# Weight chunks twice as wide, one scale per pair, one bias tile fewer kept, and the first attention tiles in another order

## The chip, the cores and the metric

The kernel runs on one core of a Trainium2 chip. The metric is the device time of one execution in microseconds (us); the kernel before takes 711.8 us as the median of three runs (711.26 to 712.23). Engines are called as the profile calls them: PE multiplies matrices and PEld loads its weights, DVE is VectorE, ACT is ScalarE, POOL is GpSimd, and SP issues most of the DMAs.

## The reference, cut to what matters

Attention with a learned relative bias for 4 batches, 8 heads and 576 positions of 64 numbers, then a feed-forward network (FFN) on 2304 tokens, 512 wide inside and 2048 wide in the hidden layer.

```python
scores = scale * np.matmul(q, k.transpose(0, 1, 3, 2))
x = (psi_rel / psi_i)[..., None]
h = np.maximum(x @ w1 + b1, 0.0)
bias = h @ w2
scores = scores + bias.transpose(2, 0, 1)[None, :, :, :]
...
attn = attn / (np.sum(attn, axis=-1, keepdims=True) + 1e-09)
return np.matmul(attn, v).astype(np.float32)
...
h = x @ w_in
relu6 = np.clip(h + 3.0, 0.0, 6.0)
g = h * relu6 / 6.0
return (g @ w_out).astype(np.float32)
```

The two FFN weights arrive as 64-bit floats, read as pairs of 32-bit words.

## The kernel before, in words

**Bias.** The bias table is made in 36 groups of 16 query rows. `z_group` builds four z tiles per group (a maximum on DVE, L840, or a Relu on ACT, L844), `bias_mm` multiplies them by w2 on PE (L857), `bias_out` scales the result on ACT (L873), and a DMA stores it in DRAM. `load_bias` fetches a table of 128 query rows and two heads for a softmax. `KEEP` lists tables that stay in the core's memory for all four batches.

**Weights.** `w_in_prep` and `w_out_prep` each take a weight in 16 chunks of 128 rows by 512 columns. A chunk is loaded (L244), its magnitude taken on ACT (L256), its mantissa word cleared down to the sign on POOL (L258), and the three instructions of `f64_pack` on DVE make one 32-bit float of each pair: clip with a row maximum (L273), shift and put the sign in (L277), put the low bits in (L280). Then `split_w` writes a high half on ACT (L121) and a low half on DVE (L138), both 16 bits wide. `row_scale` (L206 to L211) finds a power of two per row: for w_out per chunk, for w_in per four chunks. While w_in is packed, the memory of w_out (`wo`) holds its 32-bit floats.

**Attention.** A tile is 128 queries of one head; there are 144, numbered n, in units of four or five per pair of heads. Its scores (L520 or L542) get the bias and a row minimum on DVE (L554, `soft_max`), the exponential on ACT (L565), and a transpose. The first units of batches 0 and 1 are direct: PE transposes them (L613), and `pv_first` multiplies by v in 32-bit floats (L655).

**FFN.** `ffn` makes 16 hidden banks h_ps (L772, 12 multiplications each), a short chain on ACT and DVE after each (L762, L755, L749, L751), and four output banks o_ps (L795). The first call starts at tile 21 and waits between its halves until w_out is ready.

**Order.** The main loop writes the work tile by tile; rates in `CFG` say how many steps of w_in (`rwi`, `rw0`, `rw1`), w_out (`ro`), bias (`rb`) and FFN (`rf`) go with a tile, and how many bias groups come first (`g0`). A scheduler then orders each engine's instructions. From tile 45 on, PE keeps the written order. Each engine runs its own list strictly in order.

Of the kernel before, what the change touches and what calls it, by code (L numbers as in the profile page):

```python
# [33 lines left out]
def attention_moe_kernel(  # L34
# [212 lines left out]
    def f64_abs(t, eng):  # L247
        tv = t.rearrange("p (c w) -> p c w", w=2)
        lo, hi = tv[:, :, 0], tv[:, :, 1].bitcast(F32)
        u = pools["e"].tile([128, S], F32, tag="cu", bufs=2, name="cu")[:, 0:512]  # L250
        if eng == "Q":
            nc.gpsimd.tensor_scalar(
                out=u, in0=hi, scalar1=F64_BIAS, scalar2=1.0, op0=ALU.mult, op1=ALU.mult
            )
        else:
            nc.scalar.activation(out=u, in_=hi, func=AF.Abs, scale=F64_BIAS)  # L256
        if eng in "PQ":
            nc.gpsimd.tensor_scalar(  # L258
                out=hi, in0=hi, scalar1=0.0, scalar2=1.0, op0=ALU.mult, op1=ALU.mult
            )  # L260
        else:
            nc.scalar.activation(out=hi, in_=hi, func=AF.Copy, scale=0.0)
        return tv, u, eng == "Q"

    def f64_pack(tv, u, signed, dst, top):
        lo, sign = tv[:, :, 0], tv[:, :, 1]
# [1 line left out]
        if signed:
            nc.vector.tensor_reduce(
                out=top, in_=u, op=ALU.max, axis=AX.X, apply_absolute_value=True  # L270
            )
        else:
            nc.vector.tensor_scalar(  # L273
                out=u, in0=u, scalar1=F64_MAX, scalar2=0.0, op0=ALU.min, op1=ALU.max,
                accum_out=top,
            )
# [16 lines left out]
    def w_in_prep():  # L293
# [42 lines left out]
    def w_out_prep():  # L336
        top = const.tile([128, KF], F32, name="w2top")
        pw = const.tile([128, KF], F32, name="w2p")
        sw = const.tile([128, KF], F32, name="w2s")
# [3 lines left out]

        def pack(k, tu):
            f64_pack(*tu, None, col(top, k))
            row_scale(col(top, k), col(pw, k), col(sw, k))
            return tu[1]

        def high(k, u):
            split_w(wo[:, 0, k, :], wo[:, 1, k, :], u, col(sw, k), 0, pick("wm2", k))  # L350
            return u

        def low(k, u):
            split_w(wo[:, 0, k, :], wo[:, 1, k, :], u, col(sw, k), 1, pick("wm2", k))

        yield from staged(KF, [
            (0, lambda k, _: f64_load(w_out[k * 128:(k + 1) * 128, :], k)),
            (2, lambda k, t: f64_abs(t, pick("sg", k))), (3, pack), (4, high), (5, low),
        ])
# [82 lines left out]
    def split_v_b(b, p, u):  # L442
# [16 lines left out]
    def load_bias(b, p, i):  # L459
        out = b_p.tile([128, 2 * S], F32, tag="bt", name="bt")  # L460
        src = [out[:, s * S:(s + 1) * S] for s in range(2)]
        if (p, i) in KEEP:
# [3 lines left out]
            if tag != "cu":  # L466
                t = (const if tag[0] == "k" else pools["e"]).tile(
                    [128, 2 * S], F32, tag=tag, bufs=2 if tag == "z" else 1, name=f"k{p}{i}"
                )
                src = [t[:, s * S:(s + 1) * S] for s in range(2)]  # L470
            else:
                src = [
                    pools["e"].tile(
                        [128, S], F32, tag=tag, bufs=2, name=f"k{p}{i}"
                    )
                    for s in range(2)
                ]
# [757 lines left out]
```

## Time and profile before

| what | value |
|---|---|
| median of three runs | 711.8 us |
| profiled execution, its own time | 715.4 us |
| its span, first to last instruction | 713.6 us |
| PE busy | 660.9 us (93%) |
| DVE busy | 499.6 us (70%) |
| ACT busy | 491.6 us (69%) |
| POOL busy | 257.8 us (36%) |

Busy time is the time in which an engine has at least one instruction running. The shares are means over a span whose stages differ; the rows further below split it. A window row gives, for a stretch of the span, each engine's busy time and number of instructions, TensorE's granted clock as a share of full speed, and what the DMA engines did.

### The profile page before, as it was taken

To read this page: it belongs to the slowest core of one execution; us is meant where nothing else is said; L and a number is where in the kernel's file an instruction comes from. 1 tells how busy PE (TensorE), PEld (TensorE's weight loads), DVE (VectorE), ACT (ScalarE), POOL (GpSimd) and SP (SyncE) were. 2 spreads that over 40 slices of the span, in tenths; PEclk is the share of its full clock that TensorE was granted. 3 is DMA by queue.
4 is the path that set the end of the run, shared out by engine and by line. 5 is a ranking of instruction groups with operands and counts; after the bars stand their busy time and mean duration, and the time that the engine had idled before them with its cause. 6 is when DMAs were issued, how large, how long until landed. Compare 5 with 4: busy or idle time off the path is not lost. (4 is left out here: it accounts for less than half of the span.)

```text
span 713.6 us, 15332 instructions
## 1 busy us (share of the span) xinstructions
PE 660.9 (93%) x5538; PEld 470.7 (66%) x5538; DVE 499.6 (70%) x1263; ACT 491.6 (69%) x994; POOL 257.8 (36%) x350
## 2 busy tenths in 40 slices
PE   6557998998889998999999899999999999999998
PEld 2113665775456676788787688767776777777775
DVE  7999997889787697758867786777777776310310
ACT  6886887789576698758867786788568854630530
POOL 3212122345122154336643463465335611430420
PEclk9897999899799999999999999999999999999999
DMA  8985996456586987999999898967896765000000
GB/s 280 323 273 179 401 304 199 163 185 142 178 220 153 231 203 189 232 225 197 277 218 266 130 221 174 216 148 184 188 192 135 175 143 111 2 10 28 1 11 28
DMA packets 177500, 127.34 MB, mean 178 GB/s; under 512 B 138000, under 2 KB 146448, under 8 KB 177424
## 3 DMA queue, kind: packets, MB, share of 16 engines
q1 hardware_dynamic: 167632, 111.02, 63.5%
q10 hardware_dynamic: 9792, 15.34, 6.8%
q8 instruction: 43, 0.70, 0.4%
q14 instruction: 33, 0.27, 0.1%
HBM read 74.43 MB, written 15.34 MB: 126 GB/s over the span
## 5 line engine op out<-in xcount | busy, mean ns | idle before, releaser
L772 PE MATMUL h_ps<-x,wi 128*128 128x256 f16 (+1 forms) x1536 | 200.4, 288 | 9.9 <-DVE t L755 5.1
L795 PE MATMUL o_ps<-g,wo 128*128 128x256 f16 (+1 forms) x1536 | 196.2, 286 | 0.9 <-ACT g L121 0.8
L772 PEld LDWEIGHTS <-wi 128*128 128x128 f16 x1536 | 147.8, 98 | 57.3 <-issue 13.2
L795 PEld LDWEIGHTS <-wo 128*128 128x128 f16 x1536 | 147.2, 98 | 46.9 <-issue 10.0
L565 ACT ACTIVATE bt<-bt,sm 128x576 f32<-128x576 f32 x144 | 110.6, 768 | 57.0 <-DVE sm L554 55.5
L751 POOL TENSOR_TENSOR g<-t,g 128x256 f16<-128x256 f32 (+1 forms) x128 | 100.8, 797 | 133.1 <-ACT g L749 132.3
L138 DVE SCALAR_TENSOR_TENSOR hl<-bt,sm,hl 128x576 f16<-128x576 f32 x112 | 99.9, 902 | 26.2 <-POOL hl L115 14.6
L755 DVE SCALAR_TENSOR_TENSOR t<-t,t,h_ps 128x320 f32<-128x320 f32 (+1 forms) x112 | 56.1, 516 | 67.2 <-ACT t L762 66.3
L857 PE MATMUL b_ps<-z,w_sb 128*32 128x288 f32 x576 | 68.8, 441 | 22.5 <-ACT z L844 19.1
L115 POOL TENSOR_SCALAR hl<-bt,sm 128x576 f16<-128x576 f32 x56 | 49.7, 888 | 104.8 <-DVE sm L577 44.0
L749 ACT ACTIVATE g<-t 128x256 f16<-128x256 f32 (+1 forms) x128 | 55.5, 440 | 38.0 <-DVE t L755 37.1
L404 POOL TENSOR_TENSOR qkl<-st,qkh 128x576 fp32r<-128x576 f32 (+2 forms) x48 | 56.9, 1206 | 43.5 <-ACT qkh L397 42.2
L762 ACT ACTIVATE t<-h_ps,t,hr 128x320 f32<-128x320 f32 (+1 forms) x112 | 64.5, 587 | 7.0 <-PE h_ps L772 6.3
L554 DVE CUSTOM_DVE_ANT_0 bt<-s_ps,bt 128x576 f32<-128x576 f32 x80 | 58.8, 750 | 7.8 <-PE s_ps L542 6.7
L857 PEld LDWEIGHTS b_ps<-z,w_sb 128*32 128x32 f32 x576 | 20.5, 113 | 58.6 <-ACT z L844 32.6
L805 ACT ACTIVATE ot<-o_ps,os 128x256 f32<-128x256 f32 (+1 forms) x32 | 15.9, 497 | 57.2 <-PE o_ps L795 54.5
L840 DVE TENSOR_SCALAR z<-T,nbp 128x576 f32<-128x576 f32 x85 | 51.0, 640 | 4.6 <-PE b_ps L857 4.5
L844 ACT ACTIVATE z<-T,bp 128x576 f32<-128x576 f32 x59 | 45.2, 769 | 12.4 <-PE b_ps L857 8.6
L554 DVE CUSTOM_DVE_ANT_0 bt<-s_ps,k 128x576 f32<-128x576 f32 x64 | 46.1, 752 | 7.2 <-PE s_ps L542 5.2
L121 ACT ACTIVATE hl<-bt,sm 128x576 f16<-128x576 f32 x56 | 43.1, 769 | 7.5 <-DVE sm L577 1.9
L520 PE MATMUL s_ps<-qk 128*128 128x288 f32 x128 | 42.0, 455 | 5.9 <-DVE xr L682 3.0
L573 DVE TENSOR_SCALAR sm<-sm 128x1 f32<-128x1 f32 x112 | 16.7, 149 | 41.9 <-ACT bt L565 41.6
(118 smaller groups left out, 879.5 us busy)
## 6 DMA issues: line engine op xcount, KB each, us to landing
bt<-bias SPq DMA_DIRECT2D x32, 576.0 KB, 5.3
bias<-bo ACTq DMA_DIRECT2D x36, 288.0 KB, 4.1
w<-in_w_in_dram SPq DMA_DIRECT2D x16, 512.0 KB, 5.7
vs<-in_vp_dram SPq DMA_DIRECT2D x24, 320.0 KB, 4.9
st<-in_qk_dram SPq DMA_DIRECT2D x16, 448.0 KB, 4.0
wo<-in_w_out_dram SPq DMA_DIRECT2D x10, 512.0 KB, 7.1
bt<-bias SPq DMA_DIRECT2D x16, 288.0 KB, 3.8
k<-bias SPq DMA_DIRECT2D x7, 576.0 KB, 5.1
```

The lines of the kernel that those rows point to most:

```text
L138: nc.vector.scalar_tensor_tensor(out=out, in0=full, scalar=scale, in1=high, op0=ALU.mult, op1=ALU.subtract)
L404: nc.gpsimd.tensor_sub(out=lo[:, c:c + w], in0=t[:, c:c + w], in1=hi[:, c:c + w].bitcast(F32))
L554: nc.vector.tensor_tensor_reduce(out=halves(bt), in0=ps, in1=halves(src), op0=ALU.add, op1=ALU.min, scale=-0.125, scalar=3.0e38, accum_out ...
L565: nc.scalar.activation(out=bt, in_=bt, func=AF.Exp, scale=-1.0, bias=sm[:, 0:1], accum_out=total)
L749: nc.scalar.activation(out=g[:, 0], in_=uu, func=AF.Copy)
L751: e.tensor_sub(out=g[:, 1], in0=uu, in1=g[:, 0])
L755: nc.vector.scalar_tensor_tensor(out=t_t[f], in0=t_t[f], scalar=cols(f)[2], in1=h_t.pop(f)[:, 0:n], op0=ALU.min, op1=ALU.mult,)
L762: nc.scalar.activation(out=t_t[f], in_=h_t[f][:, 0:n], func=AF.Relu, scale=cols(f)[0], bias=cols(f)[1],)
L772: nc.tensor.matmul(out=h_t[f][:, 0:n], lhsT=wi[:, a, c, f * 128:(f + 1) * 128], rhs=x[:, e, c], start=(k == 0), stop=(k == 3 * KC - 1),)
L795: nc.tensor.matmul(out=ops[:, 0:n], lhsT=wo[:, a, f, e * 128:(e + 1) * 128], rhs=g_t[f][:, r], start=(f == 0 and a == 0 and r == 0), stop= ...
L840: nc.vector.tensor_scalar(out=z, in0=src, scalar1=nbp[:, col], scalar2=None, op0=ALU.max)
L857: nc.tensor.matmul(out=pss[a][32 * k:32 * k + 32, 0:HALF], lhsT=w2_sb, rhs=z[:, a * HALF:(a + 1) * HALF],)
```

## The change

Both weights are taken in half as many chunks of twice the size: w_in in 8 chunks of 1024 columns, w_out in 8 pairs of 128-row chunks. Each instruction of the packing and splitting covers 1024 columns. A pair of w_out chunks shares one scale per row, so the tables that hang on it have 8 columns instead of 16. The loads of w_in go through two buffers of 2048 words in place of five of 1024. w_in is packed in place in `wo`; for w_out the working tile is `cu` or the kept-tile slot `kb1`, and its loads go to both planes of a quarter of `wo` or to `z_e`.

The z tiles of the bias are two fixed tiles, `z_e` and `z_a`, each for a whole group. Bias table (2, 1) is not kept any more; batches 1 to 3 load it again. The first eight tiles go two by two over head pairs 0 and 1. Eight bias groups come ahead of the loop in place of 16, the others two at a time inside it; w_in's and w_out's rates are lower at first. `pv_first` takes a bank of the pool that h_ps uses in place of the pool of the scores.

```diff
-CFG = {'z0': 'AD', 'gz': 12, 'z1': 'AD', 'gz2': 16, 'zeng': 'DDA', 'sg': 'P', 'wm1': 'A', 'wm2': 'A', 'hl': 'AP', 'gl': 'PP', 'vm': 'A', 'g0': 16, 'rwi': 3.0, 'rw0': 1.0, 'rw1': 1.3, 'ro': 1.3, 'rb': 1.7, 'rf0': 1.3, 'rf': 2.0, 'rf1': 1.55, 'la': 6, 'gq': 2, 'gap': 0.0, 'wu': 8, 'act': 'o', 'w64': 5, 'rfo': 2.3, 'tv': 'A', 'pw': 0, 'po': 0, 'gr': 'AD', 'wb': 3, 'fb': 2, 'spn': 45, 'sw': 45, 'bo': 16, 'rb0': 1.5}
+CFG = {'z0': 'AD', 'gz': 12, 'z1': 'AD', 'gz2': 16, 'zeng': 'DDA', 'sg': 'P', 'wm1': 'A', 'wm2': 'A', 'hl': 'AP', 'gl': 'PP', 'vm': 'A', 'g0': 8, 'rwi': 2.0, 'rw0': 0.3, 'rw1': 0.7, 'ro': 0.85, 'rb': 1.7, 'rf0': 1.3, 'rf': 2.0, 'rf1': 1.55, 'la': 6, 'gq': 2, 'gap': 0.0, 'wu': 8, 'act': 'o', 'g1': 2, 'w64': 5, 'rfo': 2.3, 'tv': 'A', 'pw': 0, 'po': 0, 'gr': 'AD', 'wb': 3, 'fb': 2, 'spn': 45, 'sw': 45, 'ws': 2, 'os': 11, 'ro2': 2.0, 'bo': 12, 'rb0': 1.5}
...
-            t = pools["w"].tile([128, 1024], U32, tag="w64", bufs=cfg["w64"], name="w64")
-        elif k < 8 or k in (10, 11):
-            a, c = k % 2, 8 + 4 * (k // 2 % 2)
-            t = wo[:, a, c:c + 4, :].rearrange("p k e -> p (k e)").bitcast(U32)
+            t = pools["w"].tile([128, 2048], U32, tag="w64", bufs=2, name="w64")
+        elif k % 3 == 2 or k == 7:
+            t = z_e.bitcast(U32)[:, :, 0:1024]
         else:
-            t = pools["e"].tile([128, 2 * S], U32, tag="z", bufs=2, name="w64")[:, 0:1024]
+            c = 8 + 4 * (k % 3 if k < 6 else 1)
+            t = wo[:, :, c:c + 4, :].rearrange("p a k e -> p a (k e)").bitcast(U32)
...
         def at(k):
-            return k // 4, slice(512 * (k % 4), 512 * (k % 4) + 512)
+            return k // 2, slice(1024 * (k % 2), 1024 * (k % 2) + 1024)
...
-        yield from staged(16, [
-            (0, load), (2, lambda k, t: f64_abs(t, pick("sg", k))), (3, pack), (7, high), (8, low),
+        yield from staged(8, [
+            (0, load), (1, sign), (2, pack),
+            (4, lambda k, _: split(k, 0)), (5, lambda k, _: split(k, 1)),
         ])
...
+        def split(k, u):
+            ks = slice(2 * k, 2 * k + 2)
+            for step in range(2):
+                split_w(wo[:, 0, ks, :], wo[:, 1, ks, :], u, col(sw, k), step, pick("wm2", k))
+
+        ws = cfg["ws"]
+        yield from staged(KF // 2, [
+            (0, load_early), (ws - 1, load_late), (ws, sign), (ws + 1, pack), (ws + 2, split),
         ])
...
-        (0, 1): "kb0", (2, 1): "kb1",
+        (0, 1): "kb0",
...
-    tiles = [(b, p, t) for b, p, u in units for t in UT[u]]
+    tiles = [(0, p, t) for ts in ((0, 1), (2, 3)) for p in range(2) for t in ts]
+    tiles += [(b, p, t) for b, p, u in units[2:] for t in UT[u]]
...
-        ps = s_bank("pv_ps")
+        ps = halves(w_bank("pv_ps"))
...
-            fs = slice(f, f + 1)
+            fs = slice(f // 2, f // 2 + 1)
...
+                z2 = (z_a if phase == 0 and g % 2 else z_e)[:, k // 2]
...
-            bias_until(256 if i < 2 else S)
+            bias_until(128 * i + 128 if i < 2 else S)
...
+        for _ in range(cfg["g1"]):
+            if emitted[0] < 16:
+                bias_next()
...
-            ao[0] += cfg["ro"]
+            ao[0] += cfg["ro"] if out_steps[0] < cfg["os"] else cfg["ro2"]
```

The start of attention, on DVE: the rows that stand around the first softmax (`bt,sm<-s_ps,bt`) of the kernel before. `w_438` to `w_494` are loaded chunks of w_in, z is the bias, `wo` is w_in's 32-bit form and `w1p`, `w1s` its scales.

```order
L277 SCALAR_TENSOR_TENSOR cu<-cu,w_466 128x512
L313 TENSOR_REDUCE w1top<-w1parts 128x1
L280 SCALAR_TENSOR_TENSOR wo<-w_466,cu 128x512
L206 TENSOR_SCALAR w1p<-w1top 128x1
L840 TENSOR_SCALAR z<-T,nbp 128x576
L273 TENSOR_SCALAR cu,w1parts<-cu 128x512
L161 TENSOR_SCALAR w1p<-w1p 128x1
L277 SCALAR_TENSOR_TENSOR cu<-cu,w_494 128x512
L211 RECIPROCAL w1s<-w1p 128x1
L273 TENSOR_SCALAR cu,w1parts<-cu 128x512
L280 SCALAR_TENSOR_TENSOR wo<-w_494,cu 128x512
L554 ISA bt,sm<-s_ps,bt 128x576
```

The same place of the changed kernel, on DVE, where `w_276` and `w_341` are the third and fourth of the eight wide chunks of w_in.

```order
L263 TENSOR_SCALAR wo,w1parts<-wo 128x1024
L266 SCALAR_TENSOR_TENSOR wo<-wo,w_276 128x1024
L139 SCALAR_TENSOR_TENSOR wi<-wo,w1s,wi 128x1024
L837 TENSOR_SCALAR z_a<-T,nbp 128x576
L269 SCALAR_TENSOR_TENSOR wo<-w_276,wo 128x1024
L139 SCALAR_TENSOR_TENSOR wi<-wo,w1s,wi 128x1024
L554 ISA bt,sm<-s_ps,bt 128x576
L554 ISA sm 128x1
L263 TENSOR_SCALAR wo,w1parts<-wo 128x1024
L178 TENSOR_REDUCE vparts<-vf 128x1
L837 TENSOR_SCALAR z_e<-T,nbp 128x576
L266 SCALAR_TENSOR_TENSOR wo<-wo,w_341 128x1024
```

The first softmax moved from behind 13 of w_in's 16 chunks to behind three of its eight; the rest of w_in now stands between the first tiles.

The end of w_in and the start of w_out, on DVE, in the kernel before: `wi` is w_in's finished halves, and the clip into `w2top` is the first of w_out.

```order
L138 SCALAR_TENSOR_TENSOR wi<-wo,w1s,wi 128x512
L554 ISA bt,sm<-s_ps,bt 128x576
L554 ISA sm 128x1
L138 SCALAR_TENSOR_TENSOR wi<-wo,w1s,wi 128x512 x2
L157 COPY p_v_773<-m_ps 128x1
L157 COPY p_w_794<-m_ps 128x1
L138 SCALAR_TENSOR_TENSOR wi<-wo,w1s,wi 128x512
L273 TENSOR_SCALAR cu,w2top<-cu 128x512
```

The same place of the changed kernel, on DVE.

```order
L139 SCALAR_TENSOR_TENSOR wi<-wo,w1s,wi 128x1024 x2
L158 COPY p_v_777<-m_ps 128x1
L162 TENSOR_SCALAR p_v_777<-p_v_777 128x1
L184 RECIPROCAL s_v_780<-p_v_777 128x1
L682 TENSOR_TENSOR xr<-pv_ps,xr 128x256
L554 ISA bt,sm<-s_ps,bt 128x576
L554 ISA sm 128x1
L682 TENSOR_TENSOR xr<-pv_ps,xr 128x256
L554 ISA bt,sm<-s_ps,bt 128x576
L554 ISA sm 128x1
L153 TENSOR_REDUCE g_w_858<-m_ps 1x1
L263 TENSOR_SCALAR cu,w2top<-cu 128x1024 x2
```

The first w_out chunk stood right behind w_in's last half. The first two wide chunks of w_out now stand ten rows behind it; their loads go to both planes of `wo`, where w_in's last two 32-bit chunks lie until that last row of `wi` has read them.

The seventh chunk of w_in, `w_572`, on DVE in the changed kernel. It is loaded into the buffer of `w_431`, the fifth; the rows begin with the instruction that reads `w_431` last.

```order
L269 SCALAR_TENSOR_TENSOR wo<-w_431,wo 128x1024
L139 SCALAR_TENSOR_TENSOR wi<-wo,w1s,wi 128x1024
L158 COPY p_v_626<-m_ps 128x1
L139 SCALAR_TENSOR_TENSOR wi<-wo,w1s,wi 128x1024
L263 TENSOR_SCALAR wo,w1parts<-wo 128x1024
L162 TENSOR_SCALAR p_v_626<-p_v_626 128x1
L266 SCALAR_TENSOR_TENSOR wo<-wo,w_485 128x1024
L305 TENSOR_REDUCE w1top<-w1parts 128x1
L184 RECIPROCAL s_v_629<-p_v_626 128x1
L269 SCALAR_TENSOR_TENSOR wo<-w_485,wo 128x1024
L207 TENSOR_SCALAR w1p<-w1top 128x1
L263 TENSOR_SCALAR wo,w1parts<-wo 128x1024
```

In the kernel before, a chunk's buffer came free four chunks ahead of its use; now it is one chunk ahead, and the last row above needs the load and its magnitude on ACT.

## Rows read from the trace of the kernel before

**Rows 1.** Windows: stretch in us, busy time (instructions), clock, DMA share, GB/s

```profile
0.00:61.00 61.00, 39.99 (x280) 12.73 (x280) 54.78 (x128) 48.50 (x72) 14.70 (x28) 0.92 0.84 281
61.00:118.00 57.00, 51.55 (x313) 35.07 (x314) 53.58 (x165) 45.19 (x93) 11.21 (x20) 0.94 0.77 271
118.00:206.00 88.00, 77.92 (x560) 53.90 (x557) 75.36 (x206) 64.84 (x130) 34.94 (x43) 0.90 0.64 191
...
240.00:604.00 364.00, 351.80 (x3294) 270.74 (x3294) 272.87 (x666) 270.20 (x583) 165.47 (x220) 1.00 0.88 193
604.00:714.00 110.00, 106.37 (x796) 76.27 (x793) 20.00 (x38) 38.95 (x78) 25.28 (x32) 0.99 0.05 16
```

**Rows 2.** Chain that ended last: start us, us, what

```profile
684.29 26.09 PE o_ps L795 x192
```

**Rows 3.** Who waited for whom, DVE, 61 to 240 us: total, times, longest

```profile
DVE vparts L177 <- DMA va<-in_vp_dram: 5.8, 3, 2.5
DVE wo L138 <- ACT wo L121: 4.3, 4, 2.0
```

**Rows 4.** Timeline of DVE, 65 to 69 us: start us, us, instruction

```profile
65.12 0.69 DVE L280 SCALAR_TENSOR_TENSOR wo<-w,cu 128x512 uint32<-128x512 uint32 x1
65.73 0.74 DVE L138 SCALAR_TENSOR_TENSOR wi<-wo,w1s,wi 128x512 f16<-128x512 f32 x1
66.39 0.68 DVE L273 TENSOR_SCALAR_CACHE_REDUCE cu<-cu 128x512 f32<-128x512 f32 x1
...
67.00 0.68 DVE L273 TENSOR_SCALAR_CACHE_REDUCE cu<-cu 128x512 f32<-128x512 f32 x1
...
67.60 1.29 DVE L277 SCALAR_TENSOR_TENSOR cu<-cu,w 128x512 uint32<-128x512 uint32 x2
```

**Rows 5.** Instructions of single lines on DVE: ns min/median/max, first and last start

```profile
L273 DVE TENSOR_SCALAR_CACHE_REDUCE cu<-cu x32: 665/674/686, 9.7 to 174.4; 128x512 f32<-128x512 f32 x32
L273 DVE DVE_READ_ACCUMULATOR cu<-cu x32: 71/81/84, 10.4 to 175.0; 128x1 f32 x32
L277 DVE SCALAR_TENSOR_TENSOR cu<-cu,w x22: 672/685/1149, 11.5 to 176.7; 128x512 uint32<-128x512 uint32 x22
L280 DVE SCALAR_TENSOR_TENSOR wo<-w,cu x16: 671/680/693, 13.6 to 72.3; 128x512 uint32<-128x512 uint32 x16
L138 DVE SCALAR_TENSOR_TENSOR vl<-vs,s_v,vh x24: 872/885/1383, 169.7 to 590.1; 128x640 f16<-128x640 f32 x24
L138 DVE SCALAR_TENSOR_TENSOR wi<-wo,w1s,wi x16: 734/744/1152, 29.1 to 79.9; 128x512 f16<-128x512 f32 x16
```

**Rows 6.** Timeline of DVE, small instructions at 182.6 us

```profile
182.62 0.16 DVE L211 RECIPROCAL w2s<-w2p 128x1 f32<-128x1 f32 x1
182.69 0.14 DVE L577 RECIPROCAL sm<-sm 128x1 f32<-128x1 f32 x1
```

**Rows 7.** Line L256 on ACT: ns min/median/max, first and last start

```profile
L256 ACT ACTIVATE cu<-w x22: 649/672/685, 9.0 to 169.3; 128x512 f32<-128x512 f32 x22
```

**Rows 8.** Line L244, loads of 512 KB: us from issue to landing

```profile
DMA to landing us min/median/max: 3.5/5.8/10.1
```

**Rows 9.** Timeline of SP and of ACT: a pair of w_out loads and their first reader

```profile
80.50 1.69 SPq L244 DMA_DIRECT2D wo<-in_w_out_dram  x2
...
87.71 1.24 ACT L256 ACTIVATE cu<-wo 128x512 f32<-128x512 f32 x2 [0.22 <-DMA wo<-in_w_out_dram]
```

**Rows 10.** FFN lines L772 (95 to 200 us) and L795: ns, first and last start

```profile
L772 PE MATMUL h_ps<-x,wi x192: 269/273/421, 99.8 to 182.8; 128*128 128x256 f16 x192
...
L795 PE MATMUL o_ps<-g,wo x1536: 269/291/310, 203.9 to 710.1; 128*128 128x256 f16 x96, 128*128 128x320 f16 x96
```

**Rows 11.** DMA issues: KB each, median us to landing

```profile
bt<-bias SPq DMA_DIRECT2D x32, 576.0 KB, 5.3
```

**Rows 12.** Who waited for whom, PE, 240 to 604 us: total, times, longest

```profile
PE s_ps L542 <- DVE sm L554: 4.9, 5, 1.6
PE h_ps L772 <- DVE x L138: 4.7, 3, 2.8
```

More of the change, by code (lines that the diff above doesn't have):

```diff
@@ L245, in f64_load, with f64_abs, f64_pack @@
         return t
[L247 to L254, printed above, removed]
-        else:
[L256 to L266, printed above, removed]
-        ub = u.bitcast(U32)
[L268 to L276, printed above, removed]
+    def f64_abs(t, u):
+        if len(t.shape) == 3:
+            tv, u = t.rearrange("p a (c w) -> p a c w", w=2), u.rearrange("p (a c) -> p a c", a=2)
+            lo, hi = tv[:, :, :, 0], tv[:, :, :, 1].bitcast(F32)
+        else:
+            tv = t.rearrange("p (c w) -> p c w", w=2)
+            lo, hi = tv[:, :, 0], tv[:, :, 1].bitcast(F32)
+        nc.scalar.activation(out=u, in_=hi, func=AF.Abs, scale=F64_BIAS)
+        nc.gpsimd.tensor_scalar(
+            out=hi, in0=hi, scalar1=0.0, scalar2=1.0, op0=ALU.mult, op1=ALU.mult
+        )
+        return lo, hi.bitcast(U32), u
+    def f64_pack(lo, sign, u, top):
+        ub = u.bitcast(U32)
+        nc.vector.tensor_scalar(
+            out=u, in0=u, scalar1=F64_MAX, scalar2=0.0, op0=ALU.min, op1=ALU.max, accum_out=top,
+        )
         nc.vector.scalar_tensor_tensor(
@@ L296, in w_in_prep @@
         )
-        parts = const.tile([128, 16], F32, name="w1parts")
+        parts = const.tile([128, 8], F32, name="w1parts")
         top = const.tile([128, KC], F32, name="w1top")
@@ L336, in w_out_prep, with load, load_early, load_late @@
     def w_out_prep():
-        top = const.tile([128, KF], F32, name="w2top")
-        pw = const.tile([128, KF], F32, name="w2p")
-        sw = const.tile([128, KF], F32, name="w2s")
+        top = const.tile([128, KF // 2], F32, name="w2top")
+        pw = const.tile([128, KF // 2], F32, name="w2p")
+        sw = const.tile([128, KF // 2], F32, name="w2s")
         def col(t, k):
             return t[:, k:k + 1]
+        def load(k):
+            src = w_out[256 * k:256 * k + 256, :].rearrange("(a p) e -> p a e", a=2)
+            return f64_load(src, k)
+        def load_early(k, _):
+            return load(k) if k < 6 else None
+        def load_late(k, t):
+            return load(k) if k >= 6 else t
+        def sign(k, t):
+            if k % 2:
+                u = const.tile([128, 2 * S], F32, tag="kb1", name="cu")
+            else:
+                u = pools["e"].tile([128, 2 * S], F32, tag="cu", name="cu")
+            u = u[:, 0:1024]
+            return (*f64_abs(t, u), u)
         def pack(k, tu):
-            f64_pack(*tu, None, col(top, k))
+            f64_pack(*tu[:3], col(top, k))
             row_scale(col(top, k), col(pw, k), col(sw, k))
[L347 to L358, printed above, removed]
+            return tu[3].rearrange("p (k e) -> p k e", k=2)
+        def split(k, u):
[5 more added lines that the diff above has]
+            (0, load_early), (ws - 1, load_late), (ws, sign), (ws + 1, pack), (ws + 2, split),
         ])
@@ L361, in w_out_prep @@
         for name, c in (("t3", 3.0 * CQ), ("t6", 6.0 * CQ)):
-            t = const.tile([128, KF], F32, name=name)
+            t = const.tile([128, KF // 2], F32, name=name)
             nc.vector.tensor_scalar(
@@ L465, in load_bias @@
             tag = KEEP[p, i]
-            if tag != "cu":
+            if tag == "z":
+                t = z_e[:, p // 2]
+            else:
                 t = (const if tag[0] == "k" else pools["e"]).tile(
-                    [128, 2 * S], F32, tag=tag, bufs=2 if tag == "z" else 1, name=f"k{p}{i}"
+                    [128, 2 * S], F32, tag=tag, name=f"k{p}{i}"
                 )
[L470 to L477, printed above, removed]
+            src = [t[:, s * S:(s + 1) * S] for s in range(2)]
             kept[p, i] = src
@@ L1031, in attention_moe_kernel @@
     if cfg["wu"]:
-        wz = pools["a"].tile([128, 2 * S], F32, tag="z", bufs=1, name="wz")[:, 0:S].bitcast(F16)
+        wz = z_a[:, 1, 0:S].bitcast(F16)
         nc.vector.memset(wz, 0.0)
```

42 lines of the change are left out of this document (19 added, 23 removed).

## The prediction

> **What bounds the kernel now.** I read the windows first, cut where the profile changes. In the last stretch PE is busy throughout, and from 240 to 604 us PE is busy 97% of the time [rows 1]. The chain of waits names the same engine: its last piece is 192 output multiplications in 26.09 us, 0.136 us each, with no gap [rows 2]. So from about 240 us on the end is set by how much PE work is left and when it is taken up. Before that it is not: in the first 118 us DVE is busy 54.78 of 61.00 and 53.58 of 57.00 us, PE 39.99 and 51.55, ACT less than DVE. From 118 to 206 us DVE (75.36 of 88.00) and PE (77.92) wait in turns [rows 1]. The granted clock there is 0.90 to 0.94 of full speed, so PE's busy time is partly spent at the lower level of 1.2 GHz, yet PE is waited for less than DVE. What the change saves on DVE before some 206 us therefore starts PE's long stretch earlier, nearly one for one up to 118 us; what it only moves between engines does not.
>
> **The wide instructions.** Packing and splitting are 32 each of L273, L277, L280 and L138 on DVE; they become 16 of twice the width. DVE's next instruction starts 0.61 us after L280, 0.66 after L138 and 0.61 after L273 with its readout, and two of L277 take 1.29, or 0.645 each [rows 4]. Together that is 2.525 us per chunk. The added 512 columns I price by the two widths of L138: 885 ns for 640 columns, 744 for 512, or 1.10 ns a column, 0.56 us per instruction [rows 5]. Widening four instructions costs 2.26, so a pair of chunks saves 0.27 us and 16 pairs 4.3. Of the scale instructions (three per w_out chunk) 24 go. Such a small one keeps the next waiting 0.07 us [rows 6], so 1.7 us. The lower end is 6.0 us. If each instruction's whole duration counted, a pair would save 0.674 + 0.081 + 0.685 + 0.680 + 0.744 less 2.26, or 0.60 us, 16 pairs 9.7 us [rows 5], and 24 small ones at 0.15 us 3.6 [rows 6]: 13.3 us. I take 8, nearer to the starts, since DVE is almost never idle where most of the packing stands; some of it stands where the next instruction does wait.
>
> The two rows of L277 show an overlap: 1.29 us for two of 0.685. The Trainium skill (VectorE: DVE Perf Modes, section "The DRAIN you can't avoid") says that the next instruction does not start until the one before has left the pipe, and that leaving out semaphores does not help. By that rule the saving would be the upper end, 13.3 us, and the sum below 12.2 us; the trace disagrees for these instructions, so the rule is only a rival.
>
> Beside this, DVE's low half waits for ACT's high half in w_out, 4.3 us in 4 waits [rows 3]. With half as many chunks I take 2.1 us off; the bounds are 0 and 4.3. ACT loses 32 fixed parts and POOL 16, but both have more idle time than DVE in these stretches [rows 1]: nothing, as DVE's own list covers it.
>
> **The wider loads.** This is what the change adds. A load of 512 KB took 3.5, 5.8 or 10.1 us (least, median, most) [rows 8]. A load of 1 MB is not in the trace. The nearest row is a pair of 512 KB loads issued at 80.50 whose reader on ACT had to wait 0.22 us for them, until 87.71: 7.2 us for 1 MB [rows 9]. From below it is 3.5 us and 1.9 more for the second half at 271 GB/s [rows 1, 8], or 5.4; from above 10.1 and 1.9, or 12.0. I take 7.2. Then ACT takes the magnitude, at most twice 0.672, or 1.3 us [rows 7]. So DVE gets a chunk 8.5 us after its buffer was free (6.7 to 13.3).
>
> With two buffers in place of five, what stands in DVE's list in between has to cover that. For the seventh chunk of w_in these are two halves at 1.22, three packing rows at 1.17, 1.21 and 1.17, and five small ones at 0.07: 6.3 us, so DVE waits 2.2. ACT's list is blocked as well: its reader stands ahead of exponentials, and PE's transposes wait for those. For the first pair of w_out, the eighth half (1.22) and ten instructions stand in between; at the stretch's mean of 53.58/165, or 0.32 us [rows 1], they cover 4.5 us, and DVE waits 4.0. The last pair of w_out goes through a buffer that came free late too; I count 2.2, as for w_in. Together 8.4 us. I take half, 4.2: DVE idles 3.4 us from 61 to 118 and 12.6 from 118 to 206 as it is [rows 1], and while it waits for a load the other engines catch up on what it would have waited for next. The bounds are 0 and, with loads of 12.0 us and nothing caught up, 7.0 + 8.8 + 7.0 = 22.8.
>
> The row for 512 KB is what this kernel's loads take beside each other. The Trainium skill (DMA: Bandwidth & Descriptors, section "Anatomy of one DMA — SWDGE (gpsimd) path") gives 2.0 us and the bytes at 436 GB/s, for another issuing path; by it I estimate 4.4 us for 1 MB, waits of 1 us after halving, and a sum 3 us lower. The trace disagrees: by the same formula 512 KB would take 3.2 us, and its median is 5.8.
>
> **What is moved.** The first softmax goes ahead of most of w_in. DVE was full either way, so the order alone gives nothing there: 0, with the packing behind it as the cover. It would count if PE or ACT were late for DVE; they have 17 and 15 us to spare in the first 118 us by their idle sum less DVE's [rows 1].
>
> After the last attention tile the changed order leaves 732 FFN multiplications in place of 780. These 48, at 0.136 us, are 6.5 us of PE work pulled forward. It pays only where PE would have waited: for scores 4.9 us, for x 4.7 between 240 and 604 us [rows 12]. PE's list is strict, so most waits stay; I take 1 us, bounds 0 and 6.5.
>
> The edits I cost at nothing: the first FFN call's 192 hidden multiplications are spread from 99.8 to 182.8 us, 5.2 us for each of 16 banks [rows 10], so `pv_first` in one of two banks does not hold them up; without that cover, four stays of some microseconds each. The table that is no longer kept comes back as three loads of 576 KB and 5.3 us [rows 11], asked for several tiles ahead; uncovered, 16 us. The fixed z tiles hold two groups where the pools held one and a half; the remaining 20 bias groups start some tiles later but end by the same tile.
>
> **The sum**, against the profiled execution's own 715.4 us (span 713.6 and 1.8 around it): -8.0 packing, -2.1 waits for ACT, +4.2 loads, -1.0 tail, or -6.9: 708.5. That execution stands 3.6 us above the median of 711.8; from the median, 704.9 us.
>
> **Rivals.** *A larger gain.* The fixed parts come off in full (-13.3), the waits for ACT go (-4.3), loads land early (+1.5) and the tail gives 2: -18.1, 693.7 us. For it: DVE is the fullest engine for 118 us. Against: the overlapping starts [rows 4].
>
> *Nothing.* The saving is that of the starts, -6.0 - 2.1, and the three waits for loads count in full, +8.4: 712.1 us. For it: nothing in DVE's list stands ready where it waits. Against: DVE's idle time before 206 us.
>
> *Slower.* One mechanism: the 1 MB loads through two buffers. It decides once a load takes over 10 us: then, even halved, 3 times 11.4 less the covers of 6.3, 4.5 and 6.3 come to 8.6, which is what packing and waits give. At 12.0 us, not halved, +22.8 - 8.1: 726 us. For it: 10.1 us for half the size did occur [rows 8]. Against: the pair in 7.2 us [rows 9], and 271 to 281 GB/s is moved in these stretches with DMA engines 77 to 84% busy [rows 1], so there is some room.
>
> **Chances.** My forecast, from 700 to 710.4 us, gets 0.50; the larger gain 0.20; nothing 0.12; slower 0.18. A measurement of this kernel can tell about 0.2%, 1.4 us, from no change. So faster 0.70, the same 0.12, slower 0.18. The extremes of all terms at once are 688 and 729; the range from 693 to 715 leaves out about 0.05 below and 0.13 above. The forecast's own range is 700 to 710.4.
>
> **What would show it.** The 1024-column packing rows would last about 1.2 to 1.3 us; with 1.1 the larger gain is on. Loads of w_in should land in about 7 us, and DVE's waits should show two or three of some microseconds ahead of a clip, with ACT's magnitude as the releaser; with none, that term falls. The 40 us after the end of w_in's packing should be shorter than before by less than the packing saves. The first output multiplication of the first FFN call, at 203.9 us before [rows 10], should come some 6 us earlier, and from there on the two traces should run in parallel. I am wrong if that point is as early as predicted and the end is not, or if DVE has idle time of 15 us more than before ahead of it.

## The result, and the profile after

The changed kernel takes 703.45 us (median of 4 runs, 701.48 to 705.12) against 711.72; the ratio is 0.988, 95% interval 0.9855 to 0.9906. Forecast were 704.9 and a range of 693 to 715. A later measurement gave 0.991 (0.9887 to 0.9933). The two profiles exaggerate: the execution of before lies 3.7 us above its median, that of after (701.48, span 699.5) 2.0 below, so they are 13.9 us apart where the medians are 8.3. Places and orders are read from them; sizes go by the medians.

The windows of the changed kernel, cut where [rows 1] are, with the same columns:

```profile
0.00:61.00 61.00, 40.85 (x318) 17.98 (x318) 52.73 (x108) 51.31 (x71) 13.13 (x22) 0.94 0.86 297
61.00:118.00 57.00, 50.86 (x301) 34.01 (x302) 47.83 (x120) 41.17 (x76) 10.61 (x15) 0.94 0.77 271
118.00:206.00 88.00, 78.96 (x617) 56.86 (x616) 78.81 (x182) 70.86 (x133) 41.31 (x39) 0.94 0.65 193
...
240.00:604.00 364.00, 352.76 (x3292) 270.81 (x3290) 270.48 (x662) 272.25 (x585) 159.15 (x224) 1.00 0.86 189
604.00:714.00 110.00, 92.07 (x691) 65.99 (x688) 14.37 (x27) 30.27 (x60) 19.75 (x25) 0.99 0.04 13
```

DVE is busy 8 us less in the first 118 us and 3.5 more from 118 to 206. From 240 to 604 us PE, DVE and ACT differ by at most 2.4 us (POOL by 6.3), so the time was won before 240 and kept. The end is the chain of [rows 2], only earlier:

```profile
669.99 26.09 PE o_ps L795 x192
```

What was won is hardly idle time of PE. The first row of each page, before and after:

```profile
PE 660.9 (93%) x5538; PEld 470.7 (66%) x5538; DVE 499.6 (70%) x1263; ACT 491.6 (69%) x994; POOL 257.8 (36%) x350
PE 647.4 (93%) x5538; PEld 469.3 (67%) x5538; DVE 487.8 (70%) x1159; ACT 488.6 (70%) x963; POOL 252.7 (36%) x334
```

PE is idle for 52 to 53 us in both (713.6 less 660.9, 699.5 less 647.4). Its busy time is 13.5 us shorter for the same 5,538 multiplications. The granted clock of the whole span is 0.973 and 0.980 in these two executions, by an estimate 5 us of it, about what they exaggerate. For the rest: a multiplication's record lasts 0.27 us (the median of L772 further down), yet in an unbroken row a new one comes every 0.136 us ([rows 2], 26.09 us for 192). So multiplications that stand closer together show as less busy time.

The packing and splitting lines on DVE, after; they answer [rows 5]:

```profile
L263 DVE TENSOR_SCALAR_CACHE_REDUCE wo<-wo x8: 1185/1206/1219, 12.7 to 72.2; 128x1024 f32<-128x1024 f32 x8
L266 DVE SCALAR_TENSOR_TENSOR wo<-wo,w x8: 1208/1219/1226, 14.0 to 74.1; 128x1024 uint32<-128x1024 uint32 x8
L269 DVE SCALAR_TENSOR_TENSOR wo<-w,wo x8: 1203/1216/1221, 16.0 to 77.3; 128x1024 uint32<-128x1024 uint32 x8
L139 DVE SCALAR_TENSOR_TENSOR wi<-wo,w1s,wi x8: 1261/1274/1283, 30.3 to 82.8; 128x1024 f16<-128x1024 f32 x8
```

How soon the next instruction starts, in the changed kernel's timeline of DVE at 70 and at 93 to 98 us; it answers [rows 4]:

```profile
70.17 1.28 DVE L139 SCALAR_TENSOR_TENSOR wi<-wo,w1s,wi 128x1024 f16<-128x1024 f32 x1
71.37 0.16 DVE L662 TENSOR_SCALAR r_sb<-r_sb 128x4 f32<-128x4 f32 x1
...
93.55 1.22 DVE L263 TENSOR_SCALAR_CACHE_REDUCE cu<-cu 128x1024 f32<-128x1024 f32 x1
94.69 0.08 DVE L263 DVE_READ_ACCUMULATOR cu<-cu 128x1 f32 x1
...
95.37 1.23 DVE L266 SCALAR_TENSOR_TENSOR cu<-cu,wo 128x1024 uint32<-128x1024 uint32 x1
96.52 0.14 DVE L207 TENSOR_SCALAR w2p<-w2top 128x1 uint32<-128x1 uint32 x1
...
96.71 1.21 DVE L269 SCALAR_TENSOR_TENSOR cu<-wo,cu 128x1024 uint32<-128x1024 uint32 x1
97.85 0.14 DVE L162 TENSOR_SCALAR w2p<-w2p 128x1 f32<-128x1 f32 x1
```

And in the kernel before, the row behind the two of L277 at 67.60, the last of [rows 4]:

```profile
68.81 0.15 DVE L313 TENSOR_REDUCE w1top<-w1parts 128x1 f32<-128x4 f32 x1
```

In the changed kernel the next starts come 1.20, 1.14, 1.15 and 1.14 us later: 4.63 per wide chunk. The row of the kernel before corrects the prediction: two of L277 hold the next back for 1.21 us, not for 1.29, which reaches to the end of the second. That is 0.605 each, so a narrow chunk takes 2.485 and two take 4.97. Sixteen times 0.34 is 5.4 us, and with the 24 small instructions' 1.7 it is 7.1, where 8 was taken.

Loads of the weights, 1 MB each, after; 7.2 us were taken from [rows 9]:

```profile
DMA to landing us min/median/max: 4.9/6.9/9.7
```

Who made DVE wait in the changed kernel, 61 to 240 us (total, times, longest), of the rows that have to do with the weights; it answers [rows 3]:

```profile
DVE wo L139 <- DMA wo<-in_w_out_dram: 1.7, 1, 1.7
...
DVE wo L139 <- ACT wo L122: 1.5, 2, 1.1
...
DVE cu L263 <- ACT cu L255: 0.8, 1, 0.8
```

Waits for ACT's high half fell from 4.3 to 1.5 us. Two small waits have to do with loads here (1.7 for a load of w_out, 0.8 for a magnitude on ACT), and before 61 us one of 0.5.

The first FFN call, after, against [rows 10]: its hidden multiplications end five microseconds sooner, its first output multiplication starts 12.4 us sooner, and the last one of all 14.3 sooner.

```profile
L772 PE MATMUL h_ps<-x,wi x192: 269/273/421, 103.0 to 177.8; 128*128 128x256 f16 x192
...
L795 PE MATMUL o_ps<-g,wo x1536: 269/292/310, 191.5 to 695.8; 128*128 128x256 f16 x96, 128*128 128x320 f16 x96
```

### The profile page after: what moved, and what is told of

It reads as the page before. It is cut to its first block, busy times and chain, and to the rows that moved or that the text cites. A ratio compares the mean times of both kernels' runs of the same rounds, so it can differ in the third digit from the quotient of the medians.

```text
span 699.5 us, 15122 instructions
## 1 busy us (share of the span) xinstructions
PE 647.4 (93%) x5538; PEld 469.3 (67%) x5538; DVE 487.8 (70%) x1159; ACT 488.6 (70%) x963; POOL 252.7 (36%) x334
## 5 line engine op out<-in xcount | busy, mean ns | idle before, releaser
L772 PE MATMUL h_ps<-x,wi 128*128 128x256 f16 (+1 forms) x1536 | 202.6, 290 | 8.6 <-DVE t L755 3.9
L795 PE MATMUL o_ps<-g,wo 128*128 128x256 f16 (+1 forms) x1536 | 195.5, 286 | 0.8 <-DVE g L120 0.4
L772 PEld LDWEIGHTS <-wi 128*128 128x128 f16 x1536 | 149.2, 99 | 56.2 <-issue 13.9
L795 PEld LDWEIGHTS <-wo 128*128 128x128 f16 x1536 | 147.3, 98 | 46.0 <-issue 8.3
L751 POOL TENSOR_TENSOR g<-t,g 128x256 f16<-128x256 f32 (+1 forms) x128 | 102.5, 810 | 135.9 <-ACT g L749 134.9
L116 POOL TENSOR_SCALAR hl<-bt,sm 128x576 f16<-128x576 f32 x56 | 45.0, 805 | 105.6 <-DVE sm L577 59.6
L554 DVE CUSTOM_DVE_ANT_0 bt<-s_ps,bt 128x576 f32<-128x576 f32 x88 | 64.8, 749 | 10.0 <-PE s_ps L542 5.2
L854 PE MATMUL b_ps<-z_e,w_sb 128*32 128x288 f32 x448 | 44.1, 430 | 9.9 <-ACT bo L870 4.2
L520 PE MATMUL s_ps<-qk 128*128 128x288 f32 x128 | 40.2, 439 | 7.3 <-ACT atf L616 2.6
L837 DVE TENSOR_SCALAR z_e<-T,nbp 128x576 f32<-128x576 f32 x69 | 37.8, 595 | 5.4 <-PE b_ps L854 5.4
L841 ACT ACTIVATE z_e<-T,bp 128x576 f32<-128x576 f32 x43 | 32.0, 767 | 7.9 <-PE b_ps L854 4.1
L542 PE MATMUL s_ps<-qkh 64*128 64x288 f32 x192 | 30.4, 346 | 6.6 <-DVE sm L554 6.3
L870 ACT ACTIVATE bo<-b_ps,cv_sb,isc 128x576 f32<-128x576 f32 (+1 forms) x47 | 33.2, 709 | 4.2 <-DMA at<-hl 2.2
```

The lines of the kernel that those rows point to most:

```text
L116: nc.gpsimd.tensor_scalar(out=out, in0=full, scalar1=scale, scalar2=1.0, op0=ALU.mult, op1=ALU.mult)
L542: nc.tensor.matmul(out=s_t[n + j][:, a, 0:HALF], lhsT=w[q], rhs=m[rows, cs], start=(k == 0), stop=(k == 2),)
L554: nc.vector.tensor_tensor_reduce(out=halves(bt), in0=ps, in1=halves(src), op0=ALU.add, op1=ALU.min, scale=-0.125, scalar=3.0e38, accum_out ...
L751: e.tensor_sub(out=g[:, 1], in0=uu, in1=g[:, 0])
L772: nc.tensor.matmul(out=h_t[f][:, 0:n], lhsT=wi[:, a, c, f * 128:(f + 1) * 128], rhs=x[:, e, c], start=(k == 0), stop=(k == 3 * KC - 1),)
L795: nc.tensor.matmul(out=ops[:, 0:n], lhsT=wo[:, a, f, e * 128:(e + 1) * 128], rhs=g_t[f][:, r], start=(f == 0 and a == 0 and r == 0), stop= ...
```

## Experiments

All were timed beside the kernel before, on three chips: it gave 712.17 us beside runs one to four, 712.86 beside five to eight and 712.82 beside the last four. Ratios are to it, so that kernels of different chips can be compared. Where code is changed, the scheduler also places some instructions anew before tile 45, so such a run changes more than its edit says.

**The changed kernel again**, unedited.

> The changed kernel itself, as the mark for the three kernels beside it on the same chip. It gave 703.45 us, 8.3 under the kernel before; I expect 7 to 10 under it again.

Measured: 705.71 us, ratio 0.991 (0.9887 to 0.9933), 6.5 under before.

**DVE's instructions as halves.**

```diff
-            low_part(lo, t, scale, hi)
+            for a in range(2):
...
+                low_part(h[0], h[1], scale, h[2])
...
+        for a in range(2):
+            nc.vector.scalar_tensor_tensor(
+                out=half(ub, a), in0=half(ub, a), scalar=3, in1=half(sign, a),
...
+            nc.vector.scalar_tensor_tensor(
+                out=half(ub, a), in0=half(lo, a), scalar=29, in1=half(ub, a),
...
```

Here `h` holds the halves of the low half's operands, and `half(t, a)` is the a-th 512 columns of t.

> The changed kernel with three of the four wide DVE instructions of each weight chunk (both bit operations and the low half) issued as two of 512 columns; loads, ACT, POOL and buffers stay. Theory one (DVE's fixed parts before some 200 us set the end): by the starts of before (0.645, 0.61, 0.66 us) against those of after (1.14, 1.14, 1.20), 0.35 us per chunk and 5.6 for 16; with 48 instructions at DVE's fullest place I expect 3 to 5.6 us of it at the end. If the pipe's emptying were paid by every instruction: 0.50 per chunk, 8 us. Rival (the new order of the first tiles made the gain, DVE had slack left after it): under 1.5 us.

Measured: 712.32 us, ratio 1.0016 (0.9996 to 1.0035): 6.6 us slower than the first run. That is the whole gain, for 48 instructions. With L277 at 0.605 the price by starts is 4.3, not 5.6 (0.27 us per chunk); 6.6 lies between it and the price by full durations (8).

**FFN steps across the last attention tile.** In the changed kernel, and with the sign reversed in the kernel before:

```diff
+        if n == SWITCH + 1:
+            credit -= 4.0
         if queue:
```

`credit` counts the FFN steps owed to the loop.

> The changed kernel with four FFN steps (48 multiplications, 6.5 us of PE) put off from the attention part to behind its last tile, so that 780 are left there as in the kernel before. Theory one (PE is busy at both places, and work moved between them changes little): 0 to 2 us slower, 1 as predicted. Rival (the 48 multiplications pulled forward fill waits of PE): 5 to 6.5 us slower, most of the gain.

> The kernel before with four FFN steps more taken up from tile 46 on, so that 732 multiplications are left behind the last attention tile as in the changed kernel; nothing else changes. Theory one: 0 to 2 us faster than before. Rival: 5 to 6.5 us faster.

Measured: 704.71 us (0.9896, 0.986 to 0.9933), and 711.47 (0.9998, 0.9975 to 1.002). Neither differs from its partner; by the medians both are a little faster, 1.0 and 0.7 us. Work moved between two stretches in which PE is busy is worth next to nothing.

**The old start.** The tile order, how far ahead bias tables are loaded (`la`) and the bias rows wanted are put back as well.

```diff
-'g0': 8, 'rwi': 2.0, 'rw0': 0.3, 'rw1': 0.7, ... 'g1': 2
+'g0': 16, 'rwi': 3.0, 'rw0': 0.6, 'rw1': 0.7, ... 'g1': 0
-    tiles = [(0, p, t) for ts in ((0, 1), (2, 3)) for p in range(2) for t in ts]
...
+    tiles = [(b, p, t) for b, p, u in units for t in UT[u]]
```

> The changed kernel (wide chunks, pairs, two load buffers, fixed z tiles) with the start as before: 16 bias groups ahead of the loop, seven of w_in's eight chunks packed before the first softmax, the first eight tiles in the old order. Theory one (the gain is DVE's fixed parts; the order alone gives nothing, as predicted): 0 to 2 us slower than the changed kernel, 704 to 708 us. Rival (the early first softmax made the gain): 710 us or more.

Measured: 715.07 us, 1.0041 (1.0016 to 1.0065), 9.4 slower than the first run and slower than before. My theory fails: the rival holds. The start is not quite the old one: in the trace five of w_in's eight chunks, not seven, are packed ahead of the first softmax, which starts at 49.9 us (36.9 in the first run, 61.2 in the kernel before).

**ACT and POOL as halves.**

```diff
+            for a in range(2):
...
+                high_part(h[0], h[1], scale, mode)
...
+        for a in range(2):
+            nc.scalar.activation(out=half(u, a), in_=half(hi, a), func=AF.Abs, scale=F64_BIAS)
+            nc.gpsimd.tensor_scalar(
+                out=half(hi, a), in0=half(hi, a), scalar1=0.0, scalar2=1.0, op0=ALU.mult, op1=ALU.mult
+            )
```

> The changed kernel with the magnitude and high half on ACT and the sign on POOL issued as two of 512 columns each; DVE's instructions stay wide. 32 more on ACT (2 x 0.672 us against 1.15 for the magnitude, some 6 us in all), 16 more on POOL. Theory one (only DVE is waited for there): 0 to 1.5 us slower. Rival (each chunk is a chain through ACT, POOL and DVE, so any of them counts): 3 to 6 us slower.

Measured: 710.74 us, 0.9973 (0.9947 to 1.0000), 5 slower by the medians, 4.5 by the ratios. That is the rival's number, on engines costed at nothing; whether by the rival's mechanism is not shown.

**The scale of w_out sooner**, an entry of `CFG` alone.

```diff
-'ro2': 2.0
+'ro2': 4.0
```

> The changed kernel with w_out's last steps, the row scale of all of w_out among them, taken four per tile in place of two (a rate of the table alone). In the changed kernel 21 us lie between w_out's last low half and the first output multiplication, 12 of them before the transposition of the scale. Theory one (this bridge decides when PE's long stretch begins): the first output multiplication 3 to 8 us earlier and the end 1 to 4 us earlier. Rival (PE has scores and hidden multiplications enough in the bridge): within 1 us.

Measured: 715.54 us, 1.0044 (1.0018 to 1.007), 9.8 slower. Neither theory had that.

**w_out sooner.**

```diff
-'ro': 0.85
+'ro': 1.0
```

> The changed kernel with w_out's first steps at one per tile in place of 0.85, so that its packing ends some two tiles sooner and the bias groups follow sooner too. Theory one (the end hangs on when w_out is ready): 1 to 5 us faster. Rival (DVE is full there, so what is pulled ahead pushes attention back by as much): within 1.5 us.

Measured: 703.38 us, 0.9868 (0.9844 to 0.9891): 2 to 3 us faster than the first run, with intervals that still touch.

By then two entries of `CFG` had moved the end by 10 us one way and 2 the other, with the same instructions. What their traces differ in most plainly is where PE has FFN work. A row here gives the first and the last start in the stretch. The seventh run, first call's hidden half, its output half, and the second call's hidden half:

```profile
L772 PE MATMUL h_ps<-x,wi x192: 269/273/418, 103.9 to 178.6; 128*128 128x256 f16 x192
...
L795 PE MATMUL o_ps<-g,wo x192: 272/273/421, 190.1 to 219.5; 128*128 128x256 f16 x192
...
L772 PE MATMUL h_ps<-x,wi x192: 272/273/421, 244.8 to 271.8; 128*128 128x256 f16 x192
```

Two gaps, 11.5 us (178.6 to 190.1) and 25.3 (219.5 to 244.8), in which PE has only attention and bias. The same for the last version below, where they are 3.3 and 6.6:

```profile
L772 PE MATMUL h_ps<-x,wi x192: 269/273/283, 101.7 to 180.0; 128*128 128x256 f16 x192
...
L795 PE MATMUL o_ps<-g,wo x192: 269/273/284, 183.3 to 215.5; 128*128 128x256 f16 x192
...
L772 PE MATMUL h_ps<-x,wi x192: 269/273/283, 222.1 to 256.4; 128*128 128x256 f16 x192
```

The gaps of all, read from such rows, with the granted clock from 175 to 210 us in the same profiled execution (us, us, share, us):

| kernel | first gap | second gap | clock | median |
|---|---|---|---|---|
| before (profiled execution) | 21.1 | 2.3 | 0.85 | 711.7 |
| changed, first run | 13.5 | 8.2 | 0.95 | 705.7 |
| DVE halves | 24.8 | 7.7 | 0.77 | 712.3 |
| FFN steps later | 13.3 | 8.0 | 0.95 | 704.7 |
| before, FFN steps ahead | 22.2 | 2.3 | 0.95 | 711.5 |
| old start | 22.2 | 10.0 | 0.82 | 715.1 |
| ACT and POOL halves | 22.2 | 7.9 | 0.80 | 710.7 |
| scale sooner | 11.5 | 25.3 | 0.85 | 715.5 |
| w_out sooner | 3.3 | 17.8 | 1.00 | 703.4 |
| DVE halves, w_out sooner | 3.6 | 18.8 | 1.00 | 709.9 |
| old start, w_out sooner | 5.2 | 19.2 | 1.00 | 715.8 |
| both gaps closed | 3.3 | 6.6 | 1.00 | 699.4 |
| before, w_out sooner | 5.3 | 12.0 | 1.00 | 708.4 |

So a new theory: the gaps (holes, in the expectations) are the price, whatever opens them. The last four runs try it with each suspect, the first gap closed by the rate of w_out.

**DVE halves and w_out sooner**: both edits above.

> DVE's three instructions as halves (as in the second run), with w_out's first steps at one per tile. Over the runs so far the end goes with the hole between the first FFN call's last hidden and first output multiplication: 13.7 us in the changed kernel, 3.3 with w_out sooner, 22 to 25 in the three slower variants and 21 before. Theory hole: with w_out sooner the hole closes here too, and the halves cost 0 to 2.5 us against the 703.4 of w_out sooner: 703 to 706. Theory DVE (the fixed parts themselves are the gain): 5 to 7 us, 708.5 to 710.5.

Measured: 709.87 us, 0.9962 (0.9943 to 0.9982), 6.5 slower than w_out sooner. The first gap is 3.6 us, and yet the price is the same as in the second run: gaps are not the whole price, and the number is the one that the theory of DVE's fixed parts gave.

**Old start and w_out sooner**: both edits above.

> The old start (16 bias groups ahead, seven w_in chunks before the first softmax, old tile order) with w_out's first steps at one per tile. Theory hole: the old start lost 9 to 11 us because the first output multiplication fell behind three more tiles; here it does not, so 703 to 707. Rival (the early softmax itself is the gain): 710 us or more.

Measured: 715.8 us, 1.0049 (1.0028 to 1.007), 12.4 slower than w_out sooner, with a first gap of 5.2. Again not the gap.

**Both gaps closed.**

```diff
-'ro': 0.85, ... 'sw': 45
+'ro': 1.0, ... 'sw': 42
```

> The changed kernel with w_out's first steps at one per tile and the switch to four FFN banks at tile 42 in place of 45, so that the second FFN call begins three tiles sooner. With w_out sooner alone the first hole is 3.3 us but 17.8 us lie between the first call's last output and the second call's first hidden multiplication. Theory hole: that closes to under 8 us, and the end comes 3 to 6 us sooner, 697 to 701. Rival (attention and bias fill PE there as well): 702 to 705.

Measured: 699.38 us, 0.9806 (0.978 to 0.9832), faster than both kernels and 4.0 faster than w_out sooner, as the theory of gaps expected: same instructions, both gaps under 7 us.

**The kernel before, w_out sooner.**

```diff
-'ro': 1.3
+'ro': 1.5
```

> The kernel before with w_out's steps at 1.5 per tile in place of 1.3; nothing else changes. Its hole is 21 us. Theory hole: the first output multiplication follows the hidden ones within 10 us and the end comes 3 to 8 us sooner, 704 to 709, without wide chunks. Rival (in the kernel before DVE is too full to have w_out ready sooner, which is what the wide chunks changed): within 2 us of before.

Measured: 708.43 us, 0.9934 (0.9913 to 0.9955). Some 4.4 us of the 8 could be had without wide chunks, by a rate that closed the first gap of the kernel before from 21.1 to 5.3 us.

Among the four kernels with the change's own instructions and start, a line through scale sooner (36.8 us of gaps) and both gaps closed (9.9) rises 0.60 us per microsecond; it puts the first run (21.7) at 706.5 and w_out sooner (21.1) at 706.1, where 705.7 and 703.4 were measured. That is an estimate: two points fix the line, and the other two lie at almost the same place. So gaps are one price, and what the halves and the old start cost comes beside it.

## Why the prediction was right, point by point

**What bounds.** Right as to the place: the end moved by what was won before 240 us, and PE's work after that is unchanged. The signs named for it came out: the first output multiplication is 12.4 us earlier where 6 were expected (the profiles exaggerate, by 5.6 us at the end), and the last one 14.3; ahead of the first DVE idles 24.6 us in place of 22.3, far from 15 more. What the prediction did not see is the form: PE waits no less in all, its multiplications stand closer together.

**The wide instructions, -8.** The size is right, by rows 7.1. By runs, undoing three of the four cost 6.6 and 6.5 us, where their starts alone give 4.3; DVE's busy time grew by 3.6 and 4.8 us (487.5 to 491.1 and 492.2 to 497.0). The upper rival (each instruction paid in full until the pipe is empty; the Trainium skill, VectorE: DVE Perf Modes, section "The DRAIN you can't avoid") would have asked for 8; by that rule's price the runs lie in between, but the rows after show the overlap again, 1.14 us to the next start of an instruction of 1.22. So some 2 us of the price are not DVE's own time, and the new placing is in it too: the first hidden multiplication comes at 110.0 us in place of 102.9, and at 110.8 in place of 102.7. Where it is lost shows from the softmax of tile 32 to that of tile 48 (first run, second run, w_out sooner, DVE halves and w_out sooner):

```profile
143.90:249.10 105.20, 95.28 (x850) 67.47 (x850) 83.34 (x206) 76.32 (x143) 38.98 (x42) 0.95 0.77 197
143.50:258.80 115.30, 102.51 (x846) 71.77 (x846) 86.25 (x220) 79.22 (x145) 36.89 (x44) 0.88 0.69 178
144.20:253.80 109.60, 102.40 (x909) 71.44 (x912) 83.14 (x211) 81.16 (x152) 41.06 (x45) 0.96 0.71 182
144.20:259.90 115.70, 103.79 (x914) 71.81 (x916) 88.97 (x227) 84.05 (x154) 38.53 (x46) 0.97 0.69 172
```

Tile 32 comes no later with the halves. Behind it the stretch is 10.1 and 6.1 us longer, with DVE busy for 2.9 and 5.8 more. In the second run's execution the clock fell from 0.95 to 0.88 as well, in the ninth it did not, so the same price was not lost in quite the same way.

**ACT and POOL at nothing.** Unproven, and likely wrong. Halving their instructions cost 4.5 to 5 us. The trace of that run has a first gap of 22.2 us in place of 13.5, which the line above would price at about 5; whether the fixed parts opened it or the scheduler's new placing did was not separated. Late packing did not open it: w_out's last low half starts at 169.4 us there and at 171.6 in the first run. The 2.1 us for ACT's high half came as 2.8.

**The wider loads, +4.2.** The landing was right (6.9 us median for 7.2), the size too large. Three waits of 2.2, 4.0 and 2.2 us were expected, 8.4 before halving. Those that name a load or a magnitude are 0.5, 0.8 and 1.7, or 3.0 in all. DVE idles more all the same, in the windows up to the 20th and the 32nd tile's softmax, before and after:

```profile
0.00:114.00 114.00, 87.54 (x557) 45.22 (x558) 105.70 (x280) 90.50 (x157) 25.91 (x48) 0.93 0.81 278
114.00:159.00 45.00, 41.95 (x295) 31.66 (x293) 36.64 (x106) 34.03 (x71) 16.45 (x21) 0.92 0.63 210
```

```profile
0.00:106.00 106.00, 81.34 (x554) 44.94 (x555) 88.57 (x204) 83.84 (x131) 21.55 (x35) 0.94 0.82 289
106.00:144.00 38.00, 33.33 (x234) 25.12 (x231) 37.70 (x76) 32.06 (x60) 18.75 (x15) 1.00 0.73 256
```

DVE idles 17.4 us up to tile 20 in place of 8.3; from there to tile 32 it idles 0.3 in place of 8.4. The net is 1 us at tile 32. Of the 9.1 more up to tile 20 only the 3.0 stand at loads of the weights. The rest stands mainly at a bias table (2.7), at `xr`, of which the FFN's input x is made (2.8), and at scores (2.0), work of attention that the new order put there. No run tried the loads alone, so what they cost stays open.

**What is moved, 0.** This step failed: "the order alone gives nothing there". Putting the old start back costs 9.4 and 12.4 us, more than the whole change gives. The reason given was that DVE was full either way. But with the old start tile 32 comes only 1.8 us later than in the first run (145.7 and 143.9 us), and tile 48 comes 11.5 later (260.6 and 249.1). With w_out sooner they are 2.6 later (146.8 and 144.2) and 11.8 later (265.6 and 253.8). So most is lost behind tile 32, where DVE is not full. From the softmax of tile 32 to that of tile 48, old start, and old start with w_out sooner:

```profile
145.70:260.60 114.90, 103.27 (x863) 72.97 (x864) 81.81 (x202) 79.25 (x147) 38.66 (x44) 0.90 0.69 177
146.80:265.60 118.80, 107.38 (x930) 75.72 (x933) 85.10 (x207) 84.02 (x156) 40.55 (x48) 0.94 0.65 167
```

Beside the same stretch of their partners above, DVE is busy for 1.5 us less and 2.0 more, and PE for 8.0 and 5.0 more, with 13 and 21 more multiplications and a clock of 0.90 for 0.95 and 0.94 for 0.96. The first gap goes with it in the one pair (22.2 us in place of 13.5) and hardly in the other (5.2 and 3.3). What in the old start does that to those tiles stays open.

**The tail, -1.** Not told from nothing: moving the 48 multiplications across the last tile changed neither kernel beyond the noise. The rival's 5 to 6.5 us are excluded.

**The sum.** It came out through terms that cancel. DVE's halves (6.6) and the start (9.4) together exceed the 6.5 us of the first run, so the two are not independent, or the rest of the change costs some 10 us: wide chunks with the old start are slower than before. Two load buffers, the fixed z tiles, the table loaded again and the bank of `pv_first` were not tried one by one, nor the new start with narrow chunks, so which of them costs or earns what is open. A rate in `CFG` alone moved the end by 2 to 10 us, so a price of 5 us from a run that also places instructions anew is no clean price of its edit. The range and the sign were earned; the closeness of 704.9 was in part luck.

## What to carry to other kernels

Price a wide instruction by the start of the next one at both widths, read to the next row and not to the end of a merged one; here the runs cost 2 us more than that. Do not cost a new order at nothing because the fullest engine stays full: ask where the strict engine, here PE, will lack its long independent work, and read the gaps between its stages. Such a gap can be worth as much as the edit, and a rate may close it: two numbers in `CFG` gave 6 us here.

## What was not expected of the hardware

TensorE's granted clock fell inside such gaps although PE was busy for most of them. PE, from 175 to 210 us, in the second run, the seventh, and the last version (both gaps closed):

```profile
175.00:210.00 35.00, 31.40 (x212) 17.89 (x213) 29.06 (x72) 26.90 (x47) 10.66 (x14) 0.77 0.84 208
```

```profile
175.00:210.00 35.00, 32.86 (x251) 22.46 (x248) 23.32 (x64) 21.31 (x39) 8.28 (x11) 0.85 0.81 194
```

```profile
175.00:210.00 35.00, 34.48 (x317) 24.37 (x319) 24.61 (x74) 24.57 (x45) 9.01 (x10) 1.00 1.04 245
```

PE is busy 31 to 34 of 35 us in all three, but runs 212, 251 and 317 multiplications. A mean of 0.77 is full speed with stays at the lower level of 1.2 GHz. In the second run the first gap, in which PE has only attention and bias, falls into two parts:

```profile
182.60:193.60 11.00, 7.99 (x77) 4.18 (x75) 7.80 (x20) 7.29 (x15) 3.90 (x5) 1.00 1.05 268
193.80:207.20 13.40, 13.16 (x56) 7.36 (x56) 10.94 (x29) 10.61 (x19) 3.00 (x5) 0.50 1.00 242
```

PE was busy for 8.0 of 11 us at full speed, then for 13.2 of 13.4 at half of it, with fewer multiplications. The busy share hides that; the clock column and the count show it.

How much of a gap's price this is differs from execution to execution: the kernel before shows 0.85 with a first gap of 21.1 us, and its version with FFN steps ahead 0.95 with one of 22.2. Over all executions the median granted clock of the whole span is 0.972 in the first run, 0.967 with the old start, 0.966 with the scale sooner and 0.980 with both gaps closed. A difference of 0.006 is some 4 us of 712, an estimate of the most that the clock can cost of the 9.4 and 9.8 us of the fifth and seventh runs. Of the price of the ninth run it explains nothing: 0.982, against 0.978 with w_out sooner.
